# Seven small products in place of a large one, beside the steps of the next chunk, in a Fourier-mixing and feed-forward kernel

## The chip, the cores and the metric

The kernel runs on one core of a Trainium2 chip. The metric is device time in microseconds (us), the median of several executions. The engines that matter here are TensorE (PE in the profile, PEld for its weight loads), VectorE (DVE), ScalarE (ACT), and SyncE (SP), whose queue issues most DMAs. Each engine runs its own instructions in order and waits for the others by semaphores.

## The reference

With x of 2048 tokens by 512 features, everything in float32:

```python
xn = layernorm(x)
a, b = xn @ Wd_re.T, xn @ Wd_im.T          # 512 x 512
s = Ws_re @ a - Ws_im @ b                  # 2048 x 2048
h = relu(xn @ w1 + b1) ** 2                # 512 x 1792
out = x + s * silu(h @ w2 + b2)            # 1792 x 512
```

## The kernel before, in words

Every float32 operand is split into a high part, made by ACT (`split_hi`, L71), and a low part, the rest, made by DVE (`split_lo`, L74), and each product is three matmul passes: high by high, high by low, low by high. Many products are also done by a seven-product scheme for 2 by 2 blocks (Strassen's, in Winograd's form): sums of blocks of both operands, seven products of half size instead of eight, and a combination of the results.

**The first product of s.** The kernel multiplies first by the sequence matrices (cos and sin) and then by the feature matrices. The 2048 tokens of the result are done in eight chunks of 256. Chunks 0 and 1 are plain products (`products`, 512-column matmuls) made while the layer norm and its sums are still being prepared. Chunks 2 to 7 are seven products: for each chunk c there are eight steps j, and step (c, j) runs 42 matmuls of 256 columns (`mm`, L311) that add up over j in PSUM. Ahead of a step, `prep` loads the raw block of the sequence matrix, and `moving` makes three sums of blocks on DVE (`sums_b`, L205 to L207) and splits three plain blocks (768 columns, tile g0) and four sums (1024 columns, tile g1). g0 and g1 have two buffers each, so prep for step n + 2 waits for PE to have finished step n. The sums tile t has two buffers, the raw blocks have three. After a chunk's last step `combine` (L247 to L257) turns the seven results into the chunk's blocks in the tile e: one copy on ACT, four additions on DVE.

**The second product of s**, called y here, is a plain product. `pq` splits a chunk's blocks into four tiles of 512 columns. `stage2` (L289) then runs, twice per chunk, 24 matmuls of 512 columns, with the feature matrices WD[0] and WD[1] (high and low parts, four blocks of 128 rows) as the moving operand. The results are copied by ACT to ysb (L302) and stored in DRAM (L304). For chunk c - 1 this lies behind steps 1 and 2 of chunk c; chunk 7's comes after the first unit of the feed-forward part. The code has it so:

```python
        if j in (1, 2):
            with tc.issue_after(unit_end if c == PLAIN else plain_end[-1]):
                stage2(c - 1, j - 1)
```

**Weight jobs.** Nine times, at steps named in `JOBS`, `make_w` (L514) loads a raw block of w1 or w2, makes the sums, splits the seven blocks in four pieces (512, 256, 512, 512 columns), and stores high and low parts in DRAM from SP's queue, for the feed-forward part.

**The feed-forward part** has 28 hidden units (`hidden`, 42 matmuls each) and 28 outer units (`outer`), with orders written by hand.

**What sets the order.** The opening (chunks 0 and 1) and the feed-forward part are under `manual_schedule`: each engine gets its instructions in program order. The steps of chunks 2 to 7 aren't: there a planner chooses the order, and DVE's instructions of several steps, jobs and combinations are interleaved. In the opening, a chain of side work (`aside`, L453) is handed out by `beside` between chunk 1's steps, some 4.2 us a step by its own estimates.

## Time and profile before

| what | value |
|---|---|
| time, median of 3 (lowest, highest) | 715.68 us (715.3, 715.81) |
| the profiled execution's own time | 715.48 us |
| its span | 713.7 us |
| granted TensorE clock | 0.999 |
| DMA traffic | 141.09 MB, mean 198 GB/s |
| chunk 2's first step starts on PE | 109.5 us |
| the first hidden unit starts on PE | 415.8 us |
| the first outer unit starts on PE, about | 567 us |

A row of a group gives the source line, the engine, the operation, output and input tiles (g stands for the parts of a block, xc for the tokens, m_b and the like for PSUM banks, yps for y's bank), the shape, the count, the busy time and the mean duration, and behind the bar the idle time before it and what ended it. A row of the time order gives start and duration in us, and in brackets the idle time before and who ended it. Matmuls are pipelined, so PE's cost of one is the distance between starts, not its duration.

### The profile page before, as it was taken

The page shows a single profiled execution, that of the slowest core. Times are in us where ns is not written, and L with a number is a line of the kernel's source. Part 1 is how long each engine was busy: PE and PEld are TensorE (multiplying, and loading weights), DVE is VectorE, ACT ScalarE, POOL GpSimd, SP SyncE. Part 2 cuts the span into 40 slices and gives each one's busy share as a digit, 9 for nine tenths or more (in the row PEclk, how much of TensorE's full clock was granted, in tenths as well). Part 3 has the DMA queues.
Part 4 walks back from the last instruction along what each step waited for, and adds up shares of the span by engine and source line. Part 5 has one row for each costly group of instructions (what it writes and reads, how often), then busy time and mean ns, then how long its engine had stood idle before and what let it go on. Part 6 is the DMA issues. An engine that isn't in the chain of part 4 may idle for free.

```text
span 713.7 us, 12685 instructions
## 1 busy us (share of the span) xinstructions
PE 706.2 (99%) x5152; PEld 665.7 (93%) x5152; DVE 584.0 (82%) x879; ACT 348.6 (49%) x472; POOL 5.2 (1%) x8
## 2 busy tenths in 40 slices
PE   9999999999999999999999999999999999999996
PEld 6778789999999999999998999999999999999996
DVE  7999838479598797797795964999998989989897
ACT  4436434334443544444543423767767764444451
POOL 0000000000000000000000000000000000101000
PEclk9999999999999999999999999999999999999999
DMA  8533423433553653844824668965634995676644
GB/s 304 183 126 122 155 100 118 163 118 133 207 193 134 236 189 107 282 147 142 295 97 141 226 252 323 362 259 205 252 120 159 350 410 204 192 222 164 221 152 144
DMA packets 55018, 141.09 MB, mean 198 GB/s; under 512 B 5040, under 2 KB 21680, under 8 KB 53680
## 3 DMA queue, kind: packets, MB, share of 16 engines
q1 hardware_dynamic: 49840, 124.56, 50.0%
q10 hardware_dynamic: 4032, 14.68, 5.2%
q0 software_dynamic: 1088, 1.05, 1.0%
q8 instruction: 40, 0.66, 0.3%
q14 instruction: 18, 0.15, 0.1%
HBM read 97.00 MB, written 43.27 MB: 197 GB/s over the span
## 4 chain that ended last, share of the span: by engine, by line
PE 95%; DVE 3%; ACT 1%; issue 1%; DMA 0%; DVEq 0%; ACTq 0%
PE m_b L311 24%; PE yps L296 13%; PE m_b_o L648 10%; PE hps L594 10%; PE pq_b L368 6%; PE hps_b L594 6%; PE m_bb L311 5%; PE m_ba L311 5%; PE m L648 3%; PE hps_ba L594 3%; PE m_bb_o L648 2%; PE m_ba_o L648 1%; PE m_bc_o L648 1%; PE hps_bb L594 1%; PE pq_bc L368 1%; PE pq_bb L368 1%
## 5 line engine op out<-in xcount | busy, mean ns | idle before, releaser
L311 PE MATMUL m_b<-g,xc 128*128 128x256 f32 x1440 | 181.0, 281 | 0.0
L311 PEld LDWEIGHTS m_b<-g,xc 128*128 128x128 f32 x1440 | 175.3, 189 | 0.2
L74 DVE TENSOR_TENSOR g<-r,g 128x768 fp32r<-128x768 f32 (+2 forms) x65 | 65.6, 1009 | 56.0 <-ACT g L71 55.9
L71 ACT ACTIVATE g<-r 128x768 fp32r<-128x768 f32 (+2 forms) x65 | 57.7, 887 | 87.0 <-PE m_b L311 49.5
L296 PE MATMUL yps<-wd,pq 128*128 128x512 f32 x384 | 93.7, 395 | 0.0
L296 PEld LDWEIGHTS yps<-wd,pq 128*128 128x128 f32 x384 | 70.5, 188 | 15.4
L648 PE MATMUL m_b_o<-w,g 128*128 128x256 f32 x588 | 75.3, 283 | 0.0
L648 PEld LDWEIGHTS m_b_o<-w,g 128*128 128x128 f32 x588 | 72.3, 191 | 0.2 <-ACT m_b_o L641 0.2
L368 PE MATMUL pq_b<-g,xc 128*128 128x512 f32 x240 | 67.1, 398 | 0.6 <-ACT xc L71 0.4
L74 DVE TENSOR_TENSOR g<-t,g 128x1024 fp32r<-128x1024 f32 x48 | 58.7, 1224 | 6.8 <-ACT g L71 6.8
L594 PE MATMUL hps<-xT,w 128*128 128x256 f32 x504 | 61.9, 282 | 0.0
L594 PEld LDWEIGHTS hps<-xT,w 128*128 128x128 f32 x504 | 60.9, 190 | 0.1
L368 PEld LDWEIGHTS pq_b<-g,xc 128*128 128x128 f32 x240 | 43.8, 188 | 13.8 <-ACT xc L71 2.6
L71 ACT ACTIVATE g<-t 128x1024 fp32r<-128x1024 f32 x48 | 50.3, 1047 | 12.3 <-PE m_ba L311 6.8
L605 ACT ACTIVATE h<-h,b1s 128x512 f32<-128x512 f32 x56 | 37.4, 716 | 18.3 <-DVE h L256 18.3
L71 ACT ACTIVATE g<-hr 128x768 fp32r<-128x768 f32 (+1 forms) x28 | 35.5, 1267 | 21.1 <-DVE hr L213 5.3
L74 DVE TENSOR_TENSOR g<-hr,g 128x768 fp32r<-128x768 f32 (+1 forms) x28 | 41.6, 1486 | 2.3 <-ACT g L71 2.2
L311 PE MATMUL m_bb<-g,xc 128*128 128x256 f32 x288 | 43.2, 283 | 0.0
L311 PE MATMUL m_ba<-g,xc 128*128 128x256 f32 x288 | 42.7, 281 | 0.0
L311 PEld LDWEIGHTS m_bb<-g,xc 128*128 128x128 f32 x288 | 39.3, 190 | 1.8
L311 PEld LDWEIGHTS m_ba<-g,xc 128*128 128x128 f32 x288 | 38.0, 189 | 0.0
L594 PE MATMUL hps_b<-xT,w 128*128 128x256 f32 x288 | 36.2, 282 | 0.0
(169 smaller groups left out, 1024.5 us busy)
## 6 DMA issues: line engine op xcount, KB each, us to landing
r<-in_ct SPq DMA_DIRECT2D x63, 512.0 KB, 3.5
hd<-h ACTq DMA_DIRECT2D x28, 512.0 KB, 4.6
hr<-hd SPq DMA_DIRECT2D x28, 512.0 KB, 4.4
w1d<-w0g SPq DMA_DIRECT2D x21, 512.0 KB, 3.4
w<-w1d SPq DMA_DIRECT2D x6, 1792.0 KB, 9.8
w<-w2d SPq DMA_DIRECT2D x4, 1792.0 KB, 10.2
y<-ysb SPq DMA_DIRECT2D x16, 256.0 KB, 2.5
fin<-y SPq DMA_DIRECT2D x16, 256.0 KB, 5.0
```

The lines of the kernel that those rows point to most:

```text
L71: nc.scalar.activation(hi, src, AF.Copy)
L74: return nc.vector.tensor_tensor(lo, src, hi.bitcast(F32), op=ALU.subtract)
L296: ins = nc.tensor.matmul(ps, PQ[c, m, k // 2][:, a_, w:w + P], WD[m, k][:, b_, :], start=n == 0, stop=n == 2 * ND * 3 - 1)
L311: ins = nc.tensor.matmul(ps[:, d * CW:(d + 1) * CW], w[:, a_, d * P:(d + 1) * P], mv(b_), start=first and d == 0 and (a_, b_) == (HI, HI), ...
L368: ins = nc.tensor.matmul(accs[c][k], w, part[c, j][:, b_, 2 * h:2 * h + 2], start=j == 0 and h == 0 and (a_, b_) == (HI, HI), stop=j == NJ ...
L594: nc.tensor.matmul(product(ms, k), W1[p][a][:, a_, q * P:(q + 1) * P], xT[c, q][:, b_, b], start=share not in first, stop=q == 1 and (a_, ...
L605: nc.scalar.activation(x_[:, s], x_[:, s], AF.Relu, bias=b1s[:, f:f + 1])
L648: nc.tensor.matmul(m[:, k * 256:(k + 1) * 256], g[:, a_, a, k * P:(k + 1) * P], W2[p][:, b_, b], start=p == 0 and k == 0 and (a_, b_) == ( ...
```

## The change

- **y by seven products, for chunks 1 to 6.** A chunk's operand (256 tokens by twice 512 features) is taken as blocks A11, A12, A21, A22, and the feature matrices likewise. Seven products of 12 matmuls of 256 columns each (`y_product`) replace the 48 matmuls of 512. All seven use one PSUM bank, two halves: products 1, 6, 7 and 4 add up in the first, and the running sum is read after each; then 2 starts anew there and 5 and 3 use the second half. `y_result` copies the first four by ACT and adds the last three on DVE. One product stands behind each step: product i of chunk c - 1 behind step i + 2 of chunk c, the last behind step 0 of chunk c + 1; in chunk 7 all are one step earlier. Chunks 0 and 7 keep `stage2`.
- **y's operands.** `y_make` makes a part or a sum at a time, one or two for each step, with two buffers (pq00, pq01) for seven parts in place of four tiles.
- **The matrix sums.** `y_sums` makes three sums of the feature matrices and one that overwrites half of WD[0], in steps of chunk 2, from reloaded raw blocks; they are kept in DRAM (TD), and `y_load` brings each of three back per chunk, into the same two buffers (wsa, wsb). The overwritten half is saved in B12D and restored in chunk 7.
- **Weight jobs.** `make_w` becomes a generator that yields after its load, its sums and each split. One job moves into the opening's side work (`w_early`); chunks 3 to 6 hold two each, spread by `JOB_STEPS`: splits in steps 2, 2, 3, 3 and 6, 6, 7 and the next step 0. High parts go through one small buffer `st`, and ACT's queue stores them; low parts overwrite the raw block, and SP stores them at the next step.
- **Buffers.** Raw blocks have two buffers and not three, t one and not two; b2s shares `st`.
- **Order.** The whole kernel is under `manual_schedule`: for each step the order on every engine is the one written.

```diff
+JOBS = 3, 4, 5, 6
+JOB_STEPS = {0: ("", "za"), 1: ("", "a"), 2: ("a", "a"), 3: ("a", "a"), 4: ("", "b"), 5: ("", "b"),
+             6: ("b", "b"), 7: ("b", "")}
+Y_ORDER = (1, 6, 7, 4, 2, 5, 3)
...
-        t = buf("t", [P, 4, CW], f"t_{key}", bufs=2)
+        t = buf("t", [P, 4, CW], f"t_{key}")
...
+        def negated(h, l, src):
+            nc.scalar.activation(h, src, AF.Copy, scale=-1.0)
+            nc.vector.scalar_tensor_tensor(l, src, -1.0, h.bitcast(F32), op0=ALU.mult, op1=ALU.subtract)
...
+        get(ta, 1, 1)
+        get(tb, 0, 1)
+        yield
+        nc.vector.tensor_tensor(ta, ta, tb, op=ALU.add)
+        negated(WD[0][:, :, HI, CW:], WD[0][:, :, LO, CW:], ta)
+        get(tb, 0, 0)
+        yield
+        nc.vector.tensor_tensor(ta, tb, ta, op=ALU.subtract)
+        split(*y_matrix(2), ta)
+        yield
+        keep(2)
+        get(tb, 1, 0)
+        yield
+        nc.vector.tensor_tensor(ta, ta, tb, op=ALU.add)
+        negated(*y_matrix(4), ta)
+        yield
+        keep(4)
+        get(tb, 0, 1)
+        get(ta, 0, 0)
+        yield
+        nc.vector.tensor_tensor(tb, tb, ta, op=ALU.subtract)
+        split(*y_matrix(1), tb)
+        yield
+        keep(1)
+        yield
...
+    def y_part(b, name, k):
+        t = y2[b][name, "parts"] = buf(f"pq0{k}", [P, 2, ND, P], f"y{b}_{name}", F32R)
+        split(t[:, HI], t[:, LO], y2[b][name])
...
+    def y_make(b, i):
+
+        if i == 0:
+            y_part(b, "A11", 0)
+            y_sum(b, "S1", "A21", "A22", ALU.add, "A21")
+        elif i == 1:
+            y_sum(b, "S2", "S1", "A11", ALU.subtract, "A11")
+            y_part(b, "S2", 1)
+        elif i == 2:
+            y_part(b, "A22", 0)
+
+            y_sum(b, "S3", "A22", "S2", ALU.subtract, "A22")
+        elif i == 3:
+            y_part(b, "S3", 1)
+            y_sum(b, "S4", "A12", "S2", ALU.subtract, "A11")
+        elif i == 4:
+            y_part(b, "A12", 1)
+        elif i == 5:
+            y_part(b, "S1", 0)
+        elif i == 6:
+            y_part(b, "S4", 1)
+
+    Y_SUMS = {6: 2, 4: 4, 5: 1}
+    Y_PRODUCTS = {1: "A11", 6: "S2", 7: "S3", 4: "A22", 2: "A12", 5: "S1", 3: "S4"}
...
+        for q, k in enumerate(v["places"]):
+            for a_, b_ in PASSES:
+                m = yw[Y_SUMS[n]][b_][:, k] if mat is None else mat[:, k, b_, w * CW:(w + 1) * CW]
+                nc.tensor.matmul(ps, g[:, a_, q], m, start=n in (1, 2, 5) and q == 0 and (a_, b_) == (HI, HI),
+                                 stop=q == ND - 1 and (a_, b_) == (LO, HI), skip_group_check=True)
...
+        if i < 4:
+            nc.scalar.activation(to, ps, AF.Copy)
+        else:
+            nc.vector.tensor_tensor(to, ps, to, op=ALU.add)
...
+            hi = buf("st", [P, 2, 256], f"w{n}hi{p}_{first}", F32R)[:, 0:src.shape[1]]
+            split(hi, src, src)
+            nc.scalar.dma_start(to[:, HI, w], hi.bitcast(F32))
+            later.append(lambda w=w, src=src: nc.sync.dma_start(to[:, LO, w], src))
+            yield 0.6
...
+    aside = chain(sums(0), (split_sums(j) for j in range(ND)), pq_parts(0), wd_split(0),
+                  sums(1), (split_sums(j) for j in range(ND, NJ)), wd_split(1), w_early())
...
     for c, j in steps:
         if j == 0:
             ms = banks(c)
         g = part.pop((c, j))
...
+        for p in ORDER:
+            a, (grp, b) = PRODUCTS[p]
+            mm(product(ms, p), XC[j][:, a], lambda b_: g[grp][:, b_, b], j == 0, j == NJ - 1)
+
+        i = j - 2 + (c == NC - 1)
+        done = (c - 2, 6) if j == 0 and c > PLAIN else (c - 1, i) if 0 <= i < 7 else None
+        if done:
+            y_product(*done)
+        stores()
+        job(c, JOB_STEPS[j][0])
         if j == NJ - 1:
             e = buf("e", [P, 4, 512], f"c{c}")
             combine(e, ms)
...
         prep()
+        if done:
+            later.extend(lambda v=v: y_put(*v) for v in y_result(*done))
+        if c == PLAIN and j in (0, 1, 3, 4, 5, 6):
+            next(t3)
+        elif c > PLAIN and i in (-1, 1, 3):
+            y_load({-1: 2, 1: 4, 3: 1}[i])
+        for i_ in ((0, 1) if c == NC - 1 and j == 0 else (i + 2,)):
+            y_make(c - 1, i_)
+        if j == NJ - 1 and c < NC - 1:
+
+            y_begin(c, e.rearrange("p (m i) (d t n) -> p (i d) m t n", m=2, d=2, t=2), (2, 3, 0, 1))
+        job(c, JOB_STEPS[j][1])
```

More of the change, by code (lines that the diff above doesn't have):

```diff
@@ L528, in fnet_gated_kernel @@
-    work = [(0, p) for p in range(NP)] + [(1, p) for p in range(NP) if p not in W2_LATE + W2_DIRECT]
-    jobs = {(c, j): work.pop(0) for c, js in JOBS.items() for j in js}
     def load_w1(p):
@@ new lines, in fnet_gated_kernel @@
+    before = None
+    for n, (c, p) in enumerate(units):
+        ahead, behind = beside.get((c, p), ((), ()))
+        go(*ahead)
+        unit = hidden(n, c, p)
+        next(unit)
+        if n == len(units) - 1:
+            m26, m4 = bank("b2", "m_b2_o0"), bank("ba", "m_ba_o0")
+            bias(m26[:, 0], 2)
+            bias(m4[:, 0], 4)
+        if before:
+            next(before)
+        next(unit)
+        go(*behind)
+        before = unit
+        if n == 0:
+            stage2(NC - 1, 0)
+            stage2(NC - 1, 1, "ba")
+        if c == 0 and p + 4 < NP:
+            load_w1(p + 4)
@@ L926, in _launch @@
+    silu(e, C21, one)
+    for f in range(REST, NP):
+        outer(m4[1], 4, ready[c, f], f, (1,))
+    times(c, e, C12)
+    step(C21, m4[1], C21, ALU.subtract, w[1])
+    silu(e, C21, two)
+    times(c, e, C21, one)
+    plus(c, e, C21, one)
+    times(c, e, C21, two)
+    plus(c, e, C21, two)
+    plus(c, e, C12)
 def _launch(arrays, out_shape):
```

546 lines of the change are left out of this document (285 added, 261 removed).

## The prediction, made before the change was run

> **What bounds the kernel now.** I read the page's busy times first, then the chain that ended last, then the busy times of one chunk, then the vector engine's (DVE's) instructions in order of time.
>
> ```profile
> span 713.7 us, 12685 instructions
> PE 706.2 (99%) x5152; PEld 665.7 (93%) x5152; DVE 584.0 (82%) x879; ACT 348.6 (49%) x472; POOL 5.2 (1%) x8
> PE 95%; DVE 3%; ACT 1%; issue 1%; DMA 0%; DVEq 0%; ACTq 0%
> ```
>
> TensorE (PE) is busy nearly throughout and carries the chain, so only PE work taken away, or a wait put into PE, can move the time. Rows of the chain (start, length, what) give the pace:
>
> ```profile
> 141.49 3.56 PE m_b L311 x30
> 146.48 3.56 PE m_b L311 x30
> 181.26 5.59 PE yps L296 x24
> 432.18 5.04 PE hps L594 x42
> ```
>
> A step of a chunk repeats every 146.48 - 141.49 = 4.99 us; a 256-column matmul takes 3.56/30 = 0.1187 us of PE, a 512-column one 5.59/24 = 0.233 us. A chunk is 8 steps and 48 wide matmuls: 39.9 + 11.2 = 51.1 us. The busy times over chunk 3 agree (stretch, its length, then PE, PEld, DVE, ACT, POOL):
>
> ```profile
> 160.60:211.70 51.10, 51.10 (x387) 48.91 (x386) 41.01 (x63) 23.00 (x32) 0.00 (x0) 1.00 0.54 186
> DVE g L74 <- ACT g L71: 64.9, 38, 6.9
> ```
>
> DVE works 41.0 us of each 51.1; its largest wait over the whole run, 64.9 us in 38 places, is for ACT's high parts, mostly where both are ahead of PE and wait for it to free a buffer. So there is slack on DVE, but only 10 us a chunk.
>
> **What the change takes from PE.** Six chunks replace 48 x 0.233 = 11.2 us by 84 x 0.1187 = 9.97 us: 1.23 us each, **7.4 us** in all, or 708.1 from the profiled execution's 715.5 (which is 0.2 under the median of 715.68). Seven eighths of 11.2 would be 9.8; the 256-column form costs the other 0.17, since 2 x 0.1187 exceeds 0.233 by 1.7%.
>
> A chunk of the changed kernel asks PE for 8 x 4.99 + 7 x 1.42 = 49.9 us. For that to be its length, DVE and ACT must keep up, now strictly in written order.
>
> **DVE's prices.** Rows in order of time (start, duration, instruction, idle before):
>
> ```profile
> 150.96 0.96 DVE L74 TENSOR_TENSOR g<-r,g 128x768 fp32r<-128x768 f32 x1 [1.14 <-ACT g L71]
> 151.93 1.23 DVE L74 TENSOR_TENSOR g<-t,g 128x1024 fp32r<-128x1024 f32 x1
> 153.19 0.69 DVE L205 TENSOR_TENSOR t<-r 128x512 f32<-128x512 f32 x1
> 153.92 0.43 DVE L206 TENSOR_TENSOR t<-t,r 128x256 f32<-128x256 f32 x1
> 154.38 0.43 DVE L207 TENSOR_TENSOR t<-t,r 128x256 f32<-128x256 f32 x1
> 393.16 2.48 DVE L337 TENSOR_TENSOR stage<-stage 128x1024 f32<-128x1024 f32 x2 [3.68 <-DMA stage<-in_xt]
> 543.99 0.42 DVE L257 TENSOR_TENSOR h<-hps_b,h 128x256 f32<-128x256 f32 x1
> 544.33 0.68 DVE L211 TENSOR_TENSOR hs<-hr 128x512 f32<-128x512 f32 x1
> 111.88 1.23 DVE L74 TENSOR_TENSOR g<-t,g 128x1024 fp32r<-128x1024 f32 x1 [2.24 <-ACT g L71]
> 113.02 1.29 DVE L74 TENSOR_TENSOR pq<-plain,pq 128x512 fp32r<-128x512 f32 x2
> ```
>
> Where the next instruction needs nothing of the last, starts lie 1.14 us apart for 1024 columns (111.88 to 113.02), 0.60 for 512 (1.29 - 0.69) and 0.34 for 256 (543.99 to 544.33). Where it does, 0.73 for 512, 0.46 for 256, 1.26 for 1024 (393.16: 2.48 - 1.22).
>
> The Trainium skill ("VectorE: DVE Perf Modes", The DRAIN you can't avoid) has eight copies take equally long with a semaphore after each and with one after the last, so that waiting for one's predecessor costs nothing extra. The trace disagrees (0.46 against 0.34), and the rows decide; what the rule would give is in rival 2.
>
> A split's handovers stand in these rows: sums on DVE, high part on ACT, low part on DVE again.
>
> ```profile
> 397.62 0.42 DVE L207 TENSOR_TENSOR stage<-stage 128x256 f32<-128x256 f32 x1
> 398.07 1.06 ACT L71 ACTIVATE xT<-stage 128x1024 fp32r<-128x1024 f32 x1 [0.81 <-DVE stage L207]
> 399.17 1.23 DVE L74 TENSOR_TENSOR xT<-stage,xT 128x1024 fp32r<-128x1024 f32 x1 [0.26 <-ACT xT L71]
> 111.73 2.19 ACT L71 ACTIVATE pq<-plain 128x512 fp32r<-128x512 f32 x4
> 64.18 0.38 ACT L71 ACTIVATE pq<-pq_bb 128x256 fp32r<-128x256 f32 x1
> 64.44 0.40 ACT L71 ACTIVATE pq<-pq_bc 128x256 fp32r<-128x256 f32 x1
> L71 ACT ACTIVATE pq<-c 128x512 fp32r<-128x512 f32 x24 | 14.4, 628 | 29.2 <-DVE c L256 13.0 <-DVE c L248 11.7 <-DVE c L257 4.6
> ```
>
> DVE to ACT takes 0.03 us, ACT to DVE 0.04; ACT's part is 1.05 (1024 columns) or 0.63 (512); free starts on ACT lie (2.19 - 0.63)/3 = 0.52 apart for 512 and 0.26 for 256.
>
> **DVE's chain over one new chunk,** once DVE is the late one:
> - prep, per step: sums 0.73 + 0.46 + 0.43 = 1.62, ACT's second high part to 2.70, low part from 2.74, next instruction at **3.88**. Eight: 31.0.
> - y's parts and sums: steps 0 and 3, 0.60 + 0.60; step 1, sum, ACT, low part, 0.69 + 0.03 + 0.63 + 0.04 + 0.60 = 1.99; step 2, 0.73 + 0.60; steps 4 to 6, 0.60: 7.5. Result adds: 3 x 0.34 = 1.0.
> - combine, now uninterrupted: 3 x 1.26 + 0.60 = 4.4.
> - two weight jobs: 2 x (0.73 + 0.46 + 0.34 + 3 x 0.60 + 0.34) = 7.3.
>
> That is 51.2 us against PE's 49.9, before any wait for DMA. One such wait is new: make_w's high parts share one buffer, stored by ACT's queue, and the next high part waits in ACT's queue for the store; DVE's low part, and the combine or prep behind it, wait too.
>
> ```profile
> 535.49 1.06 ACT L606 ACTIVATE h<-h 128x1024 f32<-128x1024 f32 x1
> 536.58 0.33 ACTq L607 DMA_DIRECT2D hd<-h  x1
> 536.96 1.71 ACT L71 ACTIVATE w<-w2raw 128x1792 fp32r<-128x1792 f32 x1 [0.40 <-ACT h L606]
> out<-z SPq DMA_DIRECT2D x2, 128.0 KB, 1.7
> y<-ysb SPq DMA_DIRECT2D x16, 256.0 KB, 2.5
> w1d<-w0g SPq DMA_DIRECT2D x7, 256.0 KB, 3.0
> r<-in_ct SPq DMA_DIRECT2D x63, 512.0 KB, 3.5
> ```
>
> Twice a chunk two splits follow each other without a prep between (steps 2 to 3, 6 to 7); the first is the 128 KB one. Counted from prep's start in step 2, ACT's high part ends at 2.70, y's copy, y's part and the small high part at 2.70 + 0.26 + 0.52 + 0.26 = 3.7, the store issues 0.03 later and lands after 1.7 (the row of that size; 3.0 is the far end) at 5.5, the next high part ends at 6.1; DVE has been free since 3.88 + 1.33 + 0.34 = 5.5. In step 6, with no copy, it is 5.8 against 3.88 + 0.34 + 0.60 + 0.34 = 5.2. With the handover some 0.7 us idle each: 1.4. **The chain is 52.6 us a chunk** (51.2 if the store is hidden, 55.2 at 3.0 us), 2.7 over PE.
>
> Of edits I cost at nothing: three loads of a sum matrix (two 512 KB each) a chunk are issued two steps, over 11 us, before use and land in 3.5 (uncovered, 3.5 each); they wait on SP for PE's product, with only loads due a step later behind them. Two raw blocks instead of three: a load goes out after one prep and is needed two preps on, over 6 us against 3.5. ACT gains some 5 us on 23.0 (3 x 0.63, four short copies for two long, eight issues of 0.4). HI stores leave SP's queue, LO stores go out a step later there, nobody waits for either soon.
>
> **Where PE stalls.** The tightest part is S3: made in step 3 after product S2 has freed its buffer, needed at the end of step 4's matmuls.
>
> ```profile
> 109.47 0.88 PE L311 MATMUL m_bb<-g,xc 128*128 128x256 f32 x6
> 83.44 2.50 DVE L276 SCALAR_TENSOR_TENSOR wd<-wdraw,wd 128x512 fp32r<-128x512 f32 x4 [0.70 <-ACT wd L275]
> 92.86 0.60 ACT L302 ACTIVATE ysb<-yps 128x512 f32<-128x512 f32 x1 [6.63 <-PE yps L296]
> 98.27 5.76 PE L296 MATMUL yps<-wd,pq 128*128 128x512 f32 x24
> w0raw<-in_w SPq DMA_DIRECT2D x7, 512.0 KB, 3.5
> ```
>
> - Chunk 1: the early weight job starts when DVE is done with wd (85.9), its load lands at 89.4, and four high parts with three landings between (2.5, 1.7, 2.5) hold ACT to 98.9; the copy of y behind them (0.60) frees the bank at about 99.5, where PE wants it at 98.27: +1.3 (0 to 3).
> - Chunk 2 starts at 109.47 on PE; DVE is free at 113.02. A matrix sum (add, ACT, low part) costs DVE 1.22 + 0.03 + 1.05 + 0.04 + 1.14 = 3.48. To S3: 3.48, then 3.88 + 3.48 + 1.20 = 8.56, 3.88 + 1.99 = 5.87, 3.88 + 1.33 = 5.21 and 3.88 + 3.48 + 0.60 = 7.96 for steps 0 to 3, 31.1 in all, so 144.1. PE is there at 109.47 + 5 x 4.99 + 2 x 1.42 = 137.3: **+6.8**. With every start free and no wait for ACT, DVE would need some 24 us and be just in time, so I take 3 to 8 as the bounds.
> - Chunk 3: S3 to S3 is 51.2 for DVE (the last matrix sum and one weight job less its last split), 49.9 for PE: +1.3. Chunks 4, 5, 6: 2.7 each, **+8.1** (1.3 to 5.3 each).
> - Chunk 7: both take 45; +0.3. At its end DVE holds the last tokens' split, then combine, add and four splits, 4.4 + 0.34 + 2.4 = 7.1 us, beside one unit of 5.04: +1.4 (0.5 to 2).
>
> Sum: 715.5 - 7.4 + 1.3 + 6.8 + 1.3 + 8.1 + 0.3 + 1.4 = **727.3 us**.
>
> **Rivals.**
> 1. PE stays the bound: DVE's chain comes out under 49.9 us a chunk, the point from which it decides, and chunk 2's handovers hide; only chunk 1's wait stays: 708.1 + 1.3 = 709.4. For it: 46.2 us of pure DVE work (41.0 + 3 x 0.60 + 4 x 0.60 + 3 x 0.34) is less than 49.9. Against it: the 3.7 left must hold eight waits of 0.35 for the second high part. The Trainium skill ("Perfetto Trace Analysis", Identifying the Most-Contended Engine) says to judge by occupancy and optimize the highest engine first; by it PE is still that engine and the time would be 708. The trace's 46.2 of 49.9 agrees as to occupancy; it shows no chunk under this order. Chance 0.12.
> 2. The gain is just eaten: stores hidden (51.2 a chunk, 1.3 x 3 = 3.9), half of chunk 2's price (3.4), 0.5 at the end: 715.9, between 712 and 719. For it: ACT is idle half the time, so each handover could be earlier than I count. Against it: the rows of the handovers leave 0.03 us. Chance 0.20, of it 0.07 faster, 0.03 same, 0.10 slower. By the skill's rule on waits every dependent start would cost the free price: 8 x 0.25 + 0.5 + 0.4 + 0.1 = 3.0 us less a chunk, 49.6, no stall in chunks 3 to 6 and some 5.5 in chunk 2, or about 717; as the rows contradict it, it has 0.02 of these 0.20.
> 3. Stores land in 3.0, as the 256 KB row has it: two waits 1.3 longer in four chunks, 10 us more, 738; DVE begins to wait where a store takes over 1.0 us. Chance 0.10.
> 4. The products don't shorten PE: they would have to take 11.2/84 = 0.133 us each instead of 0.1187; no row nears that. Within the rest.
>
> The forecast has 0.58, at 721 to 735. This kernel's measurement can tell about 0.2%, 1.4 us, from no change. Faster: 0.12 + 0.07 = 0.19; same 0.03; slower 0.58 + 0.10 + 0.10 = 0.78. The range 712 to 736 leaves out rival 1 and most of rival 3, some 0.2.
>
> **What would show it.** Right: chunks 3 to 6 last some 53 us, not 49.9; PE's waits at y's products are for DVE at L74 (S3, step 4), the largest, near 7 us, in chunk 2; DVE is busy over 85% there and its idle time is nearly all behind ACT; ACT's high parts in make_w wait for a DMA twice a chunk. Wrong: chunks of 50 us with no PE idle; PE waiting for the matrix loads; or waits of DVE for PE in every step, which would mean that it is ahead.

## The result, and the profile after

| | median us | span of the runs | ratio to before, 95% interval |
|---|---|---|---|
| before | 715.68 | 715.30 to 715.81 | |
| after | 776.36 | 774.99 to 780.62 | 1.0859 (1.0830 to 1.0889) |

The change costs 60.7 us. The forecast was 727.3, and its range ended at 736: the sign was right, the size was not. The page of the profile after, in its three lines that answer to those shown of before (span, busy times, chain):

```profile
span 775.0 us, 13341 instructions
PE 719.9 (93%) x5368; PEld 684.4 (88%) x5368; DVE 635.8 (82%) x947; ACT 363.0 (47%) x506; POOL 5.2 (1%) x8
PE 47%; DVE 21%; DMA 16%; ACT 8%; issue 6%; SPq 1%; ACTq 0%; DVEq 0%
```

PE is idle for 775.0 - 719.9 = 55.1 us where it was idle for 7.5, and half of the chain is no longer PE's. Its busy time is also 21 us above 706.2 - 7.4 = 698.8: matmuls took longer in places, at a granted clock of 0.979 over the run (0.999 before). The third term, DMA with 16%, is the one that the prediction has hardly any of.

PE's first matmul of chunks 2 to 7 and of the hidden units now stands at 115.72, 174.76, 234.36, 294.25, 353.37, 413.76 and 475.60 us. Against what PE needs for a chunk (39.9 for its steps and 1.42 for each y product in it: six in chunk 2, eight in chunk 7, else seven) the stalls are:

| | PE's need | measured | stall | predicted stall |
|---|---|---|---|---|
| ahead of chunk 2 | 109.47 (before) | 115.72 | 6.2 | 1.3 |
| chunk 2 | 48.4 | 59.0 | 10.6 | 6.8 |
| chunk 3 | 49.9 | 59.6 | 9.7 | 1.3 |
| chunk 4 | 49.9 | 59.9 | 10.0 | 2.7 |
| chunk 5 | 49.9 | 59.1 | 9.2 | 2.7 |
| chunk 6 | 49.9 | 60.4 | 10.5 | 2.7 |
| chunk 7 | 51.3 | 61.8 | 10.5 | 0.3 |
| from the hidden units on | 297.9 (before) | 299.4 | 1.5 | 1.4 |

The stalls are 68.2 instead of 19.2 us, 49.0 more, and that is the whole error of the forecast. About 48 of them are idle time of PE (55.1 - 7.5), about 21 slower matmuls. Most of the slow matmuls seem to fill time in which PE would have waited: chunk 4, at a granted clock of 0.94, takes 59.9 us, chunk 5, at 1.00, takes 59.1. The stalls are much alike in all chunks, so one chunk tells most of it. Chunk 5 in the busy times (stretch, length, then PE, PEld, DVE, ACT, POOL, the clock granted to PE, DMA share, GB/s):

```profile
293.60:352.72 59.12, 51.42 (x422) 50.08 (x420) 48.18 (x73) 24.69 (x36) 0.00 (x0) 1.00 0.64 214
```

DVE works 48.2 of 59.1 us. Its idle time, in its instructions in order of time:

```profile
315.03 0.69 DVE L220 TENSOR_TENSOR w5a<-w5a 128x512 f32<-128x512 f32 x1
...
317.33 0.68 DVE L214 TENSOR_TENSOR t<-r 128x512 f32<-128x512 f32 x1
...
320.13 1.23 DVE L82 TENSOR_TENSOR g<-t,g 128x1024 fp32r<-128x1024 f32 x1 [0.32 <-ACT g L79]
...
322.60 0.42 DVE L82 TENSOR_TENSOR w5a<-w5a,w0hi 128x256 f32<-128x256 f32 x1
325.92 0.69 DVE L82 TENSOR_TENSOR w5a<-w5a,w0hi 128x512 f32<-128x512 f32 x1 [2.90 <-ACT w0hi L79]
...
352.35 0.69 DVE L82 TENSOR_TENSOR w5b<-w5b,w0hi 128x512 f32<-128x512 f32 x1 [3.26 <-ACT w0hi L79]
```

The last two rows are the two places where splits of a weight job follow each other without a preparation between: 6.16 us, where the prediction had 1.4. The rest is eight waits of 0.32 at a second high part, 0.70 at S2 and 0.31 at the combine; without the two, the chain is 59.12 - 6.16 = 52.96 (51.2 predicted). The releaser that the row names is ACT, but ACT isn't slow; the chain of waits shows what it waits for in turn:

```profile
320.89 0.32 ACT w0hi L79
...
321.22 3.95 DMA w1d<-w0hi
...
325.26 0.64 ACT w0hi L79
...
325.92 0.69 DVE w5a L82
```

The store of the small high part is issued at 321.2 and lands 3.95 us later; until then the one buffer is taken. SyncE's queue shows what was sent just ahead of it, a raw block of 512 KB and a low part's store of 256 KB (the second of the two stores in the last row goes out only at 323.0):

```profile
319.84 0.33 SPq L203 DMA_DIRECT2D r<-in_ct  x1
320.22 3.14 SPq L510 DMA_DIRECT2D w1d<-w5a  x2
```

The list of DMA issues has 3.9 us as the median of all stores of that size (number, KB each, median us to landing), and the waits of the engines have the cost (total, places, longest):

```profile
w1d<-w0hi ACTq DMA_DIRECT2D x21, 256.0 KB, 4.6
w1d<-w0hi ACTq DMA_DIRECT2D x7, 128.0 KB, 3.9
```

```profile
ACT w0hi L79 <- DMA w1d<-w0hi: 30.7, 10, 4.3
PE y L429 <- DVE ysb L443: 11.2, 6, 1.9
PE y L429 <- ACT y_S L79: 9.7, 5, 2.5
PE yps L308 <- ACT ysb L314: 3.5, 1, 3.5
PE hps_ba L748 <- DMA w1b<-w1d: 1.3, 1, 1.3
```

PE meets DVE's lateness at y's products, as predicted for S3 (the third row; S3 waits for DVE's low part as well, 2.8 us in five places), but also in a place that the prediction hasn't got: the first of these PE rows is product S4. It accumulates onto S1's product in the same half of a bank, so it can't start before DVE has added S1's, and that add stands behind the combine and a preparation in DVE's order.

### The profile page after: what moved, and what is told of

It is laid out like the page before. It is cut to its first block, busy times and chain, and to the rows that moved or that the text cites. A ratio compares the mean times of both kernels' runs of the same rounds, so it can differ in the third digit from the quotient of the medians.

```text
span 775.0 us, 13341 instructions
## 1 busy us (share of the span) xinstructions
PE 719.9 (93%) x5368; PEld 684.4 (88%) x5368; DVE 635.8 (82%) x947; ACT 363.0 (47%) x506; POOL 5.2 (1%) x8
## 4 chain that ended last, share of the span: by engine, by line
PE 47%; DVE 21%; DMA 16%; ACT 8%; issue 6%; SPq 1%; ACTq 0%; DVEq 0%
PE m_b_o L802 9%; PE hps L748 7%; DMA w1d<-w0hi 5%; PE pq_b L548 4%; PE hps_b L748 4%; ACT g L79 4%; DMA w1b<-w1d 3%; PE m L802 3%; DVE g L82 3%; PE yps L308 3%; DMA w2d<-w1hi 2%; DVE t L214 2%; PE hps_ba L748 2%; PE m_b L454 2%; PE m_bb_o L802 2%
## 5 line engine op out<-in xcount | busy, mean ns | idle before, releaser
L79 ACT ACTIVATE g<-t 128x1024 fp32r<-128x1024 f32 x48 | 50.8, 1059 | 97.4 <-DVE t L216 96.1
L454 PE MATMUL m_bb<-g,xc 128*128 128x256 f32 x288 | 45.5, 296 | 6.4 <-ACT c L256 5.0
L429 PE MATMUL y<-wd,y_S 128*128 128x256 f32 x144 | 25.7, 332 | 22.0 <-ACT y_S L79 9.7
L429 PEld LDWEIGHTS y<-wd,y_S 128*128 128x128 f32 x144 | 21.8, 225 | 25.1 <-ACT y_S L79 10.7
```

The source lines that it names most:

```text
L79: nc.scalar.activation(hi, src, AF.Copy)
L429: nc.tensor.matmul(ps, g[:, a_, q], m, start=n in (1, 2, 5) and q == 0 and (a_, b_) == (HI, HI), stop=q == ND - 1 and (a_, b_) == (LO, HI) ...
L454: ins = nc.tensor.matmul(ps[:, d * CW:(d + 1) * CW], w[:, a_, d * P:(d + 1) * P], mv(b_), start=first and d == 0 and (a_, b_) == (HI, HI), ...
```

## The experiments

My theory after the result: DVE's chain in the written order sets the chunk, and waits for DMA and hand-overs, not work, are what made it 59 instead of 50 us. The rivals: the work itself, the matrix loads, or the written order as such. Times are of one run each unless an interval is given, and the kernel after spans 775.0 to 780.6, so a total that moves by 4 us proves little without its trace; the kernel before took 715.5 to 715.9 beside them. The columns of chunks 3 to 7 come from the traced run and are the distances between ACT's copies at the head of successive combines (ACT c<-m_bb, the first at the time in column three).

| run | us | first copy | chunk 3 | 4 | 5 | 6 | 7 |
|---|---|---|---|---|---|---|---|
| before | 715.68 | 156.79 | 51.20 | 51.04 | 51.04 | 51.04 | 51.21 |
| after | 776.36 | 173.82 | 59.89 | 59.89 | 59.12 | 60.39 | 59.20 |
| e1 | 765.94 | 174.03 | 58.21 | 56.16 | 57.75 | 57.60 | 60.02 |
| e2 | 738.07 | 173.87 | 50.25 | 50.56 | 50.57 | 50.56 | 59.87 |
| e3 | 758.40 | 168.68 | 63.90 | 54.41 | 59.33 | 50.78 | 51.01 |
| e6 | 775.02 | 172.65 | 61.48 | 60.18 | 60.45 | 59.71 | 57.14 |
| e7 | 754.59 | 171.94 | 52.90 | 53.72 | 56.58 | 54.90 | 60.32 |
| e8 | 769.47 | 167.71 | 61.40 | 59.62 | 58.71 | 59.18 | 58.70 |
| e9 | 772.30 | 173.82 | 59.40 | 60.08 | 60.38 | 59.82 | 54.67 |
| e10 | 772.51 | 173.84 | 59.48 | 59.52 | 59.52 | 58.75 | 58.97 |
| f3 | 738.25 | 167.30 | 50.95 | 52.47 | 55.13 | 55.02 | 54.64 |
| f2 | 746.24 | 178.03 | 51.03 | 52.78 | 52.64 | 54.26 | 54.64 |
| f4 | 770.75 | 177.69 | 59.28 | 57.19 | 65.91 | 47.52 | 51.89 |
| f5 | 717.22 | 155.86 | 51.15 | 51.16 | 50.40 | 50.66 | 54.63 |
| f6 | 719.48 | 156.31 | 53.63 | 52.44 | 51.55 | 51.52 | 52.74 |
| f7 | 716.79 | 156.45 | 50.37 | 51.10 | 51.36 | 50.61 | 52.29 |
| f8 | 728.46 | 155.84 | 51.87 | 52.27 | 52.24 | 55.14 | 56.78 |
| f9 | 719.68 | 155.91 | 51.29 | 51.90 | 52.25 | 51.55 | 53.64 |
| f10 | 719.28 | 156.26 | 52.10 | 51.59 | 51.25 | 53.93 | 54.00 |

### e1: no two weight splits beside each other

```diff
-JOB_STEPS = {0: ("", "za"), 1: ("", "a"), 2: ("a", "a"), 3: ("a", "a"), 4: ("", "b"), 5: ("", "b"),
-             6: ("b", "b"), 7: ("b", "")}
+JOB_STEPS = {0: ("a", "aa"), 1: ("", "a"), 2: ("", "a"), 3: ("", "a"), 4: ("b", "bb"), 5: ("", "b"),
+             6: ("", "b"), 7: ("", "b")}
```

> The weight jobs' splits are spread out, one at the end of each step, so that no two share the store buffer without a whole preparation between them; work, stores and loads stay the same. Theory (the vector engine's written order is the bound, and the two store waits of 2.9 and 3.3 us a chunk are its largest idle part): these waits go, chunks 3 to 6 fall from 59.5 to some 53.3 us, 776.4 - 4 x 6.2 = about 751 us. Rival (something else sets the chunk, such as the matrix loads or PE's waits at the combine, and the store waits only lie beside it): chunks stay above 58 us, 770 us or more.

It took 765.94: between the two. The trace says why. The spacing took out the two waits and put three in: the first two are for the job's raw block, now loaded too shortly before its sums (the second row names no releaser, but that load went out at 326.19 and landed at 332.32), the third is a high part's again (DVE in order of time, chunk 5):

```profile
305.22 0.69 DVE L220 TENSOR_TENSOR w5a<-w5a 128x512 f32<-128x512 f32 x1 [1.24 <-DMA w5a<-in_w]
...
332.39 0.69 DVE L220 TENSOR_TENSOR w5b<-w5b 128x512 f32<-128x512 f32 x1 [2.06 <-issue]
...
345.73 0.69 DVE L82 TENSOR_TENSOR w5b<-w5b,w0hi 128x512 f32<-128x512 f32 x1 [1.18 <-ACT w0hi L79]
```

57.75 less the three (4.48) is 53.3, the length that the theory gave without waits. The run doesn't decide by its time, only by this sum. No run changed the store buffer of chunks 3 to 6 alone, by giving it a second copy for instance; what the two waits cost there is read from the traces.

### e2: the jobs' work left out

```diff
+                for s, k in ((slice(0, 4), 4), (slice(4, 7), 3)):
+                    for q in (HI, LO):
+                        nc.sync.dma_start((W1D, W2D)[n][p][:, q, s], (w1, w2)[n][p][:, 0:k])
-                next(jobs[key], None)
```

> Chunks 3 to 6 make no weight parts: the raw blocks are copied from DRAM to DRAM in as many bytes stored as before, so the sums and the splits of one matrix's seven and another's one block are left out. Theory: the vector engine is rid of 7.3 us of work and 6.2 us of store waits a chunk, 59.1 - 13.5 = 45.6, so PE's 49.9 decide, with the 2 to 3 us that PE loses at each combine: chunks of some 52.5 us, 776.4 - 4 x 7 = about 748 us, and the PE waits at the y products go. Rival (loads and stores of DRAM set the pace): the traffic is still there, chunks stay above 57 us, 766 or more.

738.07, and chunks 3 to 6 at 50.3 to 50.6: PE's pace, with the bytes still moving (229 GB/s in chunk 5 where it was 214). So neither the traffic nor the matrix loads make a chunk 59 us by themselves. (The run takes away the jobs' work and their store waits together, so it doesn't tell the two apart.) Chunk 7, which has hardly any of the jobs, stays at 59.9: it has a cause of its own.

### e3: the steps given back to the planner

```diff
+    opening.__exit__(None, None, None)
     staged = {}
     for c, j in steps:
...
+    ctx.enter_context(tc.manual_schedule(engines=None))
     units = [(c, p) for c in range(NTC) for p in range(NP)]
```

> Only the steps of chunks 2 to 7 are taken out of the written order, with PE's own order kept; the same instructions, buffers and transfers. Theory (the loss is in the written order: one waiting instruction holds all behind it on ACT and DVE): the planner moves ready work ahead of the store waits, chunks near 52 us, 776.4 - 5 x 7.5 = about 739 us, lower still if chunk 2 gains too. Rival (the work itself is too much for the vector engine, or the one buffer for the stores binds in any order): chunks stay above 57 us, 766 or more.

758.40, nearer to the rival, and very uneven: 63.9 us for one chunk, 50.8 for another. (PE's order was the planner's too here, unlike what I wrote ahead.) Some of the loss goes when ready work may pass waiting work, but the order as such isn't shown to be the cause. f4 and f5, below, bear on that.

### e6: the sum matrices loaded once

```diff
-            y_load({-1: 2, 1: 4, 3: 1}[i])
+            n = {-1: 2, 1: 4, 3: 1}[i]
+            if c == PLAIN + 1:
+                y_load(n)
+                if n == 1:
+                    yw[2] = yw[4] = yw[1]
```

> The three sum matrices are loaded in chunk 3 alone, and later chunks use what is then in the buffers (so the later y blocks are not the reference's): 3 MB of loads less in each of chunks 4 to 7, the rest the same. Theory (these loads share the DMA engines with the stores and make a 128 KB store land in 3.9 instead of 1.7 us): the landing falls to some 2.5 us, each store wait by 1.4, chunks 4 to 6 from 59.8 to 57, and chunk 7 by 2, 776.4 - 3 x 2.8 - 2 = about 766 us. Rival (the landing has nothing to do with them): 3.9 us stays, 774 to 777 us.

The run leaves out the loads of chunks 4 to 7, whose products then use what chunk 3 left in the buffers. 775.02: the rival. Chunk 7 gains 2 us, the others nothing, and a small store still takes as long:

```profile
w1d<-w0hi ACTq DMA_DIRECT2D x7, 128.0 KB, 4.1
```

What makes such a store land in 4 us instead of the 1.7 of the end of the kernel is not these loads. In chunk 5 they weren't ahead of it in the kernel after either: there, as here, a raw block and a low part's store are (1.4 and 1.0 us). The 256 KB stores, which did go out behind the matrix loads, fell from 4.6 to 2.5 us, but the two waits don't hang on them.

### e7: one split a step, in the middle of the preparation

```diff
-        prep()
+        if i == -1 and c < NC - 1:
+            y_sum(c - 1, "S2", "S1", "A11", ALU.subtract, "A11")
+        prep(lambda: (job(c, JOB_STEPS[j][0]), stores()))
...
+JOB_STEPS = {0: ("z", "a"), 1: ("a", ""), 2: ("a", ""), 3: ("a", "b"), 4: ("a", "b"), 5: ("b", ""),
+             6: ("b", ""), 7: ("b", "n")}
```

> One weight split a step again, now in the middle of the preparation (between the two pairs of splits, where the vector engine waited 0.32 us for ACT), with the sums a step ahead, the next raw block loaded as soon as its buffer is free, the low part's store issued at once, and S2's sum ahead of step 1's preparation, so that its 0.70 us wait goes too. The first spacing gave 57 us a chunk because three waits for a load or a store were left in it (1.24, 2.06 and 1.18 us in chunk 5). Theory (written-order chain of the vector engine): 59.7 less 6.2 of store waits, 2.6 at the second high part and 0.7 at S2 is 50.2, so PE decides at 50.0 to 51; 776.4 - 4 x 9 = about 740 us. Rival (some other coupling, such as the combine or the matrix loads): chunks of 53 us or more, 750 or more.

754.59, in the rival's range: chunks of 52.9 to 56.6, so some 5 us a chunk came back (59.8 to 54.5 on average), but not nine. What is left is other waits. PE's in the longest chunk:

```profile
288.31 1.68 PE L430 MATMUL y<-wd,y_S 128*128 128x256 f32 x12 [1.81 <-DVE ysb L444]
307.39 0.35 PE L430 MATMUL y<-y_t,y_S 128*128 128x256 f32 x1 [0.98 <-DMA y_t<-td]
310.05 2.38 PE L430 MATMUL y<-y_t,y_S 128*128 128x256 f32 x11 [2.30 <-DMA y_t<-td]
```

56.58 less these 5.09 is 51.5. The matrix loads, harmless while DVE was late, come next: taking one wait away shows the next one.

### e8, e9: chunk 1 and chunk 7 by themselves

```diff
-            hi = buf("st", [P, 2, 256], f"w{n}hi{p}_{first}", F32R)[:, 0:src.shape[1]]
+            hi = his[:, w]
...
+        for spent in make_w(*work.pop(0), e[:, 0:4], e[:, 4:8], buf("g1b", [P, 8, 256], "w_early_hi", F32R)):
```

> Only the early weight job of chunk 1 is changed: its four high parts get a place of their own, so that ACT doesn't wait for three landings. Theory: PE's 3.53 us wait for the copy of y goes, and with it the lower clock after it, so chunk 2 starts near 110 instead of 115.7 us; the vector engine is early by as much, and the total falls by 5, to 771. Rival (chunk 2 is bound by the vector engine, whose work before it is the same): chunk 2 starts earlier and ends as before, 774 to 777. If the lower clock has nothing to do with the wait, 2 to 3 us are gained in chunk 1 and the clock stays at 0.94.

769.47. PE in order of time, the kernel after and then e8:

```profile
97.50 0.87 PE L548 MATMUL pq_ba<-g,xc 128*128 128x512 f32 x3
101.90 8.38 PE L308 MATMUL yps<-wd,pq 128*128 128x512 f32 x24 [3.53 <-ACT ysb L314]
```

```profile
97.69 0.86 PE L551 MATMUL pq_ba<-g,xc 128*128 128x512 f32 x3
98.39 5.76 PE L308 MATMUL yps<-wd,pq 128*128 128x512 f32 x24
```

The wait is gone, and with it a second cost: the same 24 matmuls took 8.38 us behind the wait and take 5.76 without it. Over that stretch of the kernel after the granted clock is 0.80 (stretch, length, PE, PEld, DVE, ACT, POOL, clock):

```profile
101.90:115.70 13.80, 13.80 (x48) 11.01 (x49) 8.28 (x13) 5.53 (x9) 0.00 (x0) 0.80 0.59 200
```

Chunk 2 starts at 109.59, the time of before. So the early job's three landings cost 3.53 + 2.62 = 6.2, where I had 1.3.

```diff
-            for q, js in ((0, (3, 4, 4)), (1, (5, 6, 6))):
+            for q, js in ((0, (4, 4, 5)), (1, (5, 6, 6))):
```

> Only the first token block's normalization and sums in chunk 7 go one step later (from the end of step 3 to step 4, its splits to step 5). Theory: the vector engine's 5.3 us wait for that load, with a preparation behind it, goes; chunk 7 falls from 61.8 to some 56.5, 776.4 - 5 = about 771 us. Rival (the work is only moved to the end, where the last splits and the first hidden unit wait for it): 775 to 778.

772.30, and chunk 7, on which the reading rests, falls from 59.2 to 54.7. The row of the kernel after that names it:

```profile
451.14 2.48 DVE L480 TENSOR_TENSOR stage<-stage 128x1024 f32<-128x1024 f32 x2 [5.32 <-DMA stage<-in_xt]
```

In the written order the next preparation stood behind that load.

### e10, f2: chunk 2's matrix sums elsewhere

```diff
-        nc.vector.tensor_tensor(ta, ta, tb, op=ALU.add)
+        nc.gpsimd.tensor_tensor(ta, ta, tb, op=ALU.add)
...
+            nc.gpsimd.tensor_tensor(l, src, h.bitcast(F32), op=ALU.subtract)
```

> Only the four sums of y's matrices in chunk 2 are changed: the adds and the low parts are made by GpSimd (idle in the kernel until the end) instead of the vector engine, a step earlier for the adds; ACT negates two of them first. Theory: the vector engine is rid of 4 x (1.22 + 1.14) = 9.4 us, 7 of them between chunk 2's first step and S3, so the 10.6 us stall of chunk 2 falls to some 3; about 769 us. Rival (GpSimd takes so long over 1024 columns, or slows the vector engine so much, that the parts come later still): chunk 2 stays at 59 us or grows, 776 to 790.

772.51, and the first copy stands where it stood, at 173.84: chunk 2 gained nothing (the 4 us of the total lie behind it, where nothing was changed). DVE, then GpSimd (POOL):

```profile
125.50 2.48 DVE L82 TENSOR_TENSOR y_A<-plain,y_A 128x512 fp32r<-128x512 f32 x1 [1.34 <-ACT y_A L79]
127.91 2.88 DVE L391 TENSOR_TENSOR plain<-plain 128x512 f32<-128x512 f32 x1
```

```profile
125.03 2.41 POOL L345 TENSOR_TENSOR wd<-y_t,wd 128x1024 fp32r<-128x1024 f32 x1 [6.03 <-ACT wd L344]
127.52 2.72 POOL L358 TENSOR_TENSOR y_t<-y_t,y_t 128x1024 f32<-128x1024 f32 x1
```

A DVE operation of 0.69 us that begins while GpSimd adds takes 2.5 to 2.9: it ends 0.55 us after GpSimd's, in all seven such places around chunk 2. Here that gave back what was taken off DVE. f2 (on top of f3) lets DMAs accumulate instead:

```diff
-        nc.vector.tensor_tensor(ta, ta, tb, op=ALU.add)
+                nc.gpsimd.dma_start(t[:, k], wd[m, :, k, half * CW:(half + 1) * CW], accum_op=ALU.add)
```

> As f3, and the four matrix sums of chunk 2 add by accumulating DMAs instead of the vector engine (ACT negates three blocks first, in place). Theory: the vector engine's chain in chunk 2 is shorter by 4 x 1.22 = 4.9 us, chunk 2 falls by 4 to 5, so some 5 below f3, about 724. Rival (such DMAs take long or hold the vector engine as GpSimd's own adds did, 2.8 us for an operation of 0.69): no gain over f3 or a loss of up to 5.

746.24, 8 above f3: the rival, at more than its price. ACT's high parts now stand in order behind such a DMA, and everything behind ACT with them:

```profile
132.08 1.06 ACT L79 ACTIVATE y_t<-y_t 128x1024 fp32r<-128x1024 f32 x1 [6.52 <-DMA y_t<-in_wd]
...
155.02 1.06 ACT L344 ACTIVATE y_t<-y_t 128x1024 f32<-128x1024 f32 x1 [6.23 <-DMA y_t<-in_wd]
```

### f3 and f4: all of it together, written and planned

f3 joins e7 (its sums a step later), e8 and e9, and:

```diff
+        if c > PLAIN and (j == 0 or i in (1, 3)):
+            y_load({1: 4, 3: 1}.get(i, 2))
+        def between():
+            if done:
+                later.extend(lambda v=v: y_put(*v) for v in y_result(*done))
+            job(c, JOB_STEPS[j][0])
+            stores()
+        prep(between)
```

> All mended orders together, the same work: weight splits one a step in the middle of the preparation with their sums beside the first of them, early job's high parts apart, staging a step later, y's copies and result adds in the middle of the preparation instead of behind it, and the sum matrices loaded as soon as PE has left their buffer. The last two answer to what the first version of this left over in chunk 4 (PE waits of 1.81 us for the add behind the combine, 0.98 and 2.30 for a matrix load). Theory (what is left of the loss in chunks 3 to 6 is such waits, no work): chunks of 50 to 51 us there, 776.4 - 4 x 9.2 - 6.9 - 4.1 = about 729, less 1 to 3 in chunks 2 and 7. Rival (the matrix loads, 1 MB in each of three, cannot come in time beside the other traffic): chunks of 53, 738 or more. Chunk 2 stays near 58 in both, since its four matrix sums are 13.9 us of the vector engine's chain.

738.25: the rival's number, for a reason close to its own: not the amount of traffic, as I read it, but its bunching (f5 takes it apart, together with other moves). Chunk 3 is at 50.95; chunks 5 and 6 are at 55, because the matrix load for S2 now stands at a chunk's start beside four other transfers, and a store among them lands late (7.9 us). DVE, then PE, in chunk 4 to 5:

```profile
292.44 0.69 DVE L220 TENSOR_TENSOR w4n<-w4n 128x512 f32<-128x512 f32 x1 [3.11 <-DMA w1d<-w4b]
```

```profile
292.36 1.00 PE L455 MATMUL m_b<-g,xc 128*128 128x256 f32 x7
296.02 4.50 PE L455 MATMUL m_b<-g,xc 128*128 128x256 f32 x23 [2.65 <-DVE g L82]
```

f4 is f2 with the edit of e3:

> As f2, with the steps of chunks 2 to 7 taken out of the written order. Theory (with waits out of the way the written order costs nothing more): within 4 us of f2, mostly through chunk 2, where the planner can take ready work first. Rival (the written order itself still costs): 8 us or more below f2, near 712. A worse time, as the first planner run's chunk 3 of 63.9 us could bring, says that the planner's own guesses are off.

770.75, 24.5 above f2: neither theory's number, but the third case that the expectation names. With the same instructions and buffers this planner's order is far worse than the written one. That doesn't clear written orders as such; f5, itself a written order, does: what an order makes wait for, and where, is what costs.

### f5 to f10: the remaining waits, one after the other

f5, on f3: S2's matrix loaded at the end of the chunk before, S1's add behind the combine, adds and splits of chunk 2's matrix sums apart.

```diff
+        elif j == NJ - 1 and c < NC - 1:
+            y_load(2)
+        if j == NJ - 1:
+            result()
...
+        if c == PLAIN and j in (0, 2, 4):
+            next(t3)
```

> As f3, with three more moves of order and none of work: the sum matrix for product S2 is loaded at the end of the chunk before (as soon as PE has left its buffer) instead of in the burst at the start of a chunk, where a store took 7.9 us to land and the vector engine waited 3.11 us for it; the result add of S1 stands right behind the combine; and in chunk 2 the adds of the matrix sums and their splits are put apart, the splits into the middle of a preparation, the two last loads a step earlier. Theory (every loss in these chunks is a wait in the written order): chunks 3 to 6 near 50.5, chunk 2 from 58.5 to 52 or less; 738.3 - 12 - 6 = about 720 us, 716 at best, where the change breaks even. Rival (24 MB more of DRAM traffic is the limit now, whatever the order): chunks stay at 53 to 55, 730 or more.

717.22 (716.13 to 720.84 over 10 runs), ratio to before 1.0029 (1.0017 to 1.0041): the theory. Chunk 2 lost its stall through order alone: the first copy went from 167.30 to 155.86, with all four sums still on DVE.

f6, on f5: staging loads ahead of the preparation, A11's and S3's parts earlier.

```diff
+            if i + 2 == 3:
+                y_make(c - 1, 3)
...
+        if c == NC - 1 and j == 0:
+            y_make(c - 1, 0)
         prep(between)
```

> As f5, with four more moves of order and none of work: the token blocks' loads in chunk 7 stand ahead of the preparation (PE has left their buffers there), so that their normalization goes back to the end of step 3; A11's part stands ahead of chunk 7's first preparation; S3's part stands in the middle of step 3's preparation. Left in f5 by its own trace: 1.7 us of PE waits where the hidden units begin, 0.6 at A11 in chunk 7, 1.3 at S3 in chunk 2 and 0.2 in three more chunks. Theory (only waits stood between the change and its 7.4 us less of PE work): 717.2 - 4 = about 713 us, faster than the kernel before by some 0.3%. Rival (what is left is the DRAM traffic and the vector engine's own work, 88% busy): 716 to 718, no faster than before.

719.48, ratio 1.0047 (1.0034 to 1.0061): no faster, as the rival says, and not told apart from f5, whose interval overlaps. The waits at S3 are gone and stand at the combine instead:

```profile
210.59 0.98 PE L459 MATMUL m_bb<-g,xc 128*128 128x256 f32 x6 [1.83 <-ACT c L256]
211.85 5.30 PE L459 MATMUL m_b<-g,xc 128*128 128x256 f32 x30 [0.28 <-DVE c L257]
...
318.51 2.36 PE L459 MATMUL m_b<-g,xc 128*128 128x256 f32 x18 [1.00 <-DVE c L265]
```

f7, on f6: S4's product inside the first step. f8, on f7: the halves of a matrix loaded a step apart.

```diff
+            if p == ORDER[2] and j == 0 and done:
+                y_product(*done)
```

> As f6; in the first step of a chunk PE runs y's product S4 after three of its seven products instead of after all, so that 1.42 us more of PE work lie between a chunk's last product and the first that needs a bank which the combine's third operation frees; the add that S4 waits for stands behind the combine's first operation. f6's trace shows PE waits of 0.7, 2.1, 1.6, 1.0 and 1.0 us there (the moves of f6 only shifted its waits to this place). Theory (waits only): 719.5 - 5 = about 714.5, level with or just under the kernel before. Rival (the wait moves on again, since the vector engine and ACT have no slack left): 718 or more.

> As f7, with the loads of a sum matrix's high and low half a step apart, so that no step issues more than one of them (f6's trace has a 256 KB store of a weight part landing after 8.8 us behind such a 1 MB load, and 4.9 us of ACT waiting for it). Theory (store landings set what is left): 1 to 3 us below f7, about 712. Rival (a low half that is loaded a step later comes too late for its product, or the total traffic is what delays the stores): no better than f7.

f7: 716.79 (714.31 to 720.06 over 12 runs), ratio 1.0018 (1.0006 to 1.0031), the lowest of the changed kernels, though its interval overlaps f5's. f8: 728.46, ratio 1.0182 (1.0165 to 1.0199); the halves come too late for their product:

```profile
196.65 1.57 PE L437 MATMUL y<-y_t,y_A 128*128 128x256 f32 x11 [2.69 <-DMA y_t<-td]
```

f9, on f7: `JOB_STEPS` one step later. f10, on f9: two matrix loads behind the step's weight store.

> As f7, with the weight jobs one step later throughout (sums and first split in steps 2 and 6 instead of 1 and 5), because f7's trace shows PE waiting 0.5 to 0.7 us a chunk in the fourth step for the vector engine, which has had no pause since the combine, and ACT waiting 1.1 us for a raw block. Theory (waits only): these go, 716.8 - 3 = about 714, faster than before by 0.2%. Rival (they move on, or what is left is the scatter of landings under this traffic: 714.3 to 720.1 over f7's runs): 716 or more.

> As f9, with the loads of two of the three sum matrices put behind the weight store of the same step instead of ahead of it. Theory (a store lands late behind 1 MB of loads): ACT's waits of 2 us for the store buffer in step 6 shrink, another 0.5 to 2 us, and the scatter over the runs becomes smaller. Rival (the loads come too late for their product then, as the halves of f8 did): slower than f9 by 2 to 10.

719.68, ratio 1.0043 (1.0029 to 1.0058), and 719.28, ratio 1.0049 (1.0036 to 1.0061): neither below f7. For f9 that is its rival; f10 is neither of its two cases, level with f9. In f9 the waits stand at the combine again. So 59.6 of the 60.7 us come back by order (and a place of its own for the early job's high parts), with the same work, and no version is faster than before in the median. The busy line of f7, from the fastest of its 12 runs, tells where that leaves the idea:

```profile
span 712.5 us, 13369 instructions
PE 700.4 (98%) x5368; PEld 671.0 (94%) x5368; DVE 631.3 (89%) x947; ACT 363.9 (51%) x506; POOL 5.2 (1%) x8
```

PE's work fell by 5.8, from 706.2 to 700.4, and its idle time rose by 4.6, from 7.5 to 12.1: in this execution, of 714.31 us, the change is 1.2 us ahead. f7's median is 2.5 us longer, which puts it about 1 us behind; its slowest run took 720.06, where before has 715.2 to 716.6 over 16 runs. Whether the rest can be moved away as well stays open: three attempts moved waits about. What makes the scatter isn't shown; the landing of stores is my guess.

## Why the prediction was wrong in size

- **PE's gain** (7.4 us): 5.8 in f7, about right.
- **DVE's chain becomes the bound in chunks 3 to 6**: right, and right in its prices. A preparation takes 3.93 (3.88 predicted), the combine 4.53 (4.4), a job's sums 1.70 (1.53); without store waits 52.96 instead of 51.2. e2 shows that the weight jobs, work and store waits together, are what lifts it over PE's.
- **The store wait** ("lands after 1.7 (the row of that size; 3.0 is the far end)"): this is the step that failed. The mechanism was named to the instruction; the landing was 3.9, outside both bounds, and the two waits 6.16 instead of 1.4. The 1.7 came from two stores at the very end of the kernel, where only the last stores of the result move; the row of the same operation that I had (3.0 for 256 KB, with traffic) was nearer in kind and I put it at the far end. With 3.95 in place of 1.7 the prediction's own sum gives about 2.9 us for each wait (2.90 and 3.26 measured). The 4.8 us that it lacks and 1.8 more of prices and hand-overs (52.96 - 51.2) are the 6.5 us by which chunk 5, at 59.1, was over the forecast's 52.6. Over chunks 3 to 6 the store waits come to 24.6 us by the traces' rows, where the forecast had 4.2: 20.4 of the 49.0 us that it lacks, the largest part. The next are chunk 7 (10.2), chunk 1 (4.9) and chunk 2 (3.8), below.
- **Chunk 3** (+1.3): I counted it from S3 to S3 and left both store waits out, though its jobs have the same two places. It stalled for 9.7.
- **Chunk 1** (+1.3): ACT's wait was seen, too short again for the same reason; and that a waiting PE runs slower afterwards was not priced at all: 3.53 + 2.62 (e8).
- **Chunk 2** (+6.8, measured 10.6): the place and the size at S3 were right. PE needs 27.8 us to S3 from its start at 115.72, so 143.5; it got there at 149.55 and waited 0.84 more inside, 6.9 in all: 2.37 + 0.84 at S3 itself, the rest in two earlier waits and slower matmuls. The other 3.7 come behind it. There DVE waits for a raw block of the last matrix sum, which landed 7.8 us after its issue and which the prediction costed at nothing; no run moved this load alone:

```profile
164.65 1.23 DVE L367 TENSOR_TENSOR y_t<-y_t,y_t 128x1024 f32<-128x1024 f32 x1 [3.48 <-DMA y_t<-in_wd]
```

  That the four sums were too much work in any order was not right: f5 has the same work without the stall.
- **Chunk 7** (+0.3, measured 10.5): "both take 45" compared work with work. The staging load, costed at nothing, is what DVE waits for (5.32), with a preparation behind it; e9 gives 4.5 us of the chunk back. What makes the rest, no run shows by itself.
- **S4 behind S1's add**: not seen. In the trace after it is PE's largest row of waits (11.2 us; S3's two rows make 12.5). As I read it, it is there how DVE's lateness reaches PE, not another cause, and costs by itself once DVE is in time (1.81 in e7); no run shows that apart.
- **The rivals**: rival 1 (PE stays the bound) was wrong, with chunks of 59 us. Rival 3 (stores at 3.0, 738) was the right one and still too mild; its 0.10 should have been the main case. The matrix loads, costed at nothing with 3.5 each if uncovered, were covered while DVE was late, and showed in e7 and f3.
- **What would show it**: ACT's high parts waiting for a DMA twice a chunk, PE waiting at S3, idle DVE behind ACT: all there. The chunk of 53, the busy share of 85% (59 and 82%) and a wait near 7 us at S3 in chunk 2 (3.2) were not.

## What to carry to other kernels

When an order is written out, price every instruction of each queue by what it waits for, not by what it does: a small store that frees a buffer two instructions ahead can cost more than all the arithmetic that a change adds. Take the price of a transfer from rows under the traffic that it will meet, above all behind the same transfers, and if only a quiet row exists, make the loaded one the main case. And when a chain has several waits, removing one shows the next: mend all that the trace shows before judging the idea.

## What the hardware showed that I had not expected

- **PE can run slower after a short wait.** From 112 to 420 us of the traces of all eighteen changed kernels I took each idle stretch of PE of 1 us or more with 30 undisturbed 256-column matmuls behind it. After stretches of 1 to 1.5 us, 2 of 31 were followed by slow matmuls; after 1.5 to 3 us, 26 of 47; after more (4.1 to 8.5 us), 4 of 4. Slow ones took 171 to 216 ns each, at a granted clock of 0.52 to 0.69; the others 121 to 126 ns, at 1.00. In f3 above, 23 matmuls behind 2.65 us take 4.50 us instead of 23 x 0.1187 = 2.7. The Trainium skill ("TensorE: Matmul & The Clock Gate", HAM oscillation — how this bites in real kernels) gives the rule "no PE-idle gaps >~3.4µs"; here gaps of half that do it, though not each time. It lengthened the kernel where PE was the bound (chunk 1); in chunk 5 the clock was 1.00 and the chunk as long as the others.
- **GpSimd's additions held DVE's operations up.** 0.69 us became 2.5 to 2.9 (e10), each ending 0.55 us after GpSimd's. The Trainium skill ("SBUF — State Buffer", Who interferes with whom) says that the two share a pair of ports under an exclusive lock; the trace agrees, with operations that read both inputs from SBUF.
- **A store's landing went with what was in flight ahead of it more than with its size.** I grouped the stores of high parts in the same eighteen traces by the transfers that had been issued before and not yet landed. Stores of 256 KB took 2.0 us (median of 88) with none in flight, and 5.7 (of 77) behind a raw block and both halves of a sum matrix. Stores of 128 KB took 1.7 (of 10, one place of chunk 1 in ten traces) behind nothing but another high part's store, and 3.85 (of 64) behind a raw block and a low part's store, the company of the two waits. This sorts traces; it is no test of one transfer alone.
